# Attention and two gated layers on one core: the first chunk of tokens as plain float32 matmuls, and x of the second layer through the weights' buffers

## The chip, the cores and the metric

The kernel runs on one core of a Trainium2 chip. The metric is the device time of one execution in microseconds (us); less is better. Engines are called as in the profile: PE (TensorE, matmuls), PEld (its weight loads), DVE (VectorE), ACT (ScalarE), POOL (GpSimd) and SP (SyncE, which here only issues transfers).

## The reference

Block-causal attention, then two dense layers. Inputs are drawn as float32 or, where the host keeps them in double precision, float64.

```python
def _attn_ref(q, k, v):                       # q, k, v: (4, 8, 576, 64)
    scores = scale * np.matmul(q, k.transpose(0, 1, 3, 2))
    mask = block_i >= block_j                 # blocks of 64 positions
    scores = np.where(mask, scores, -1000000000.0)
    ...
    return np.matmul(attn, v)

def _moe_ref(x, w1, w2, w3, w_out):           # x: 2304 x 512, w: 512 x 768
    h = np.maximum(np.maximum(x @ w1, x @ w2), x @ w3)
    return h @ w_out                          # 768 x 512

def _moe2_ref(x, w_gate, w_val, w_out):       # 512 x 1536, 1536 x 512
    gate = 1.0 / (1.0 + np.exp(-(x @ w_gate)))
    return gate * (x @ w_val) @ w_out
```

## The kernel before

**Weights.** All weights arrive in 64-bit words, 128 x 512 words a piece (512 KB): 24 pieces `wa` of layer 1 (18 of the experts w1 to w3, 6 of w_out) and 36 pieces `wb` of stage 2, as the second layer is called here. A piece is turned into float32 on chip: ACT rescales the high word (L671), DVE shifts the low word (L675) and joins the two (L679). The joined float32 value then lies in every second 32-bit word of the tile. Since matmuls run in the fast type fp32r, which keeps fewer bits, every operand is split: ACT casts the high part (L691), DVE subtracts it for the low part (L90, tile `w` or `WB`). A product takes three matmuls: high x high, high x low, low x high (L511 to L513 for the experts, L549 to L551 for the projection with w_out, L1002 to L1004 for gate and value, L982 to L984 for the output).

**Where the pieces lie.** Single pieces go through a ring of four buffers (`raw_p`, tile `wraw`), which comes free with the low part. In front, 15 pieces of layer 1 are loaded three at a time into the places of weights that are not made yet (`land_unit`, tile `wland`, 1.5 MB; five units, u from 2 to 6).

**Layer 1 and attention.** Attention is 32 jobs (a batch and a pair of heads, once for its first 256 tokens and once for the other 320). Layer 1 goes in eight chunks: four of 256 tokens, then four of 320. Chunk i needs the four jobs that make its tokens, and runs beside the next four. Per chunk there are 18 groups `experts(i, f, w)` (f of six blocks of h, w of three matrices; 12 matmuls each), their maximum (`larger`: ACT copies the first, L520, DVE takes the maximum with the second and third, L522), the split of h (`high_h` on ACT, L533, `low_h` on DVE), and 4 groups `project(i, d, fs)` of 18 matmuls, whose result goes to DRAM (`x2d`).

**The order.** Jobs, weights and chunks are written as `Op`s with an engine, a cost, what they wait for, the ring they take a buffer from and a due time. `plan()` runs a list scheduler over them: it gives each engine the ready Op that is due first, with 1.9 us from a load's end to its reader and 370 GB/s on the wire. `run_plan()` then emits everything in the order of the planned starts, and that order is kept on PE, DVE, ACT and SP. The chip waits where the plan was wrong; it doesn't reorder.

**Stage 2.** Six chunks of 384 tokens, 12 steps f each. A step is 24 matmuls into `ps_g` and `ps_v`, a sigmoid (ACT), a product `gv` (DVE, L1009) and its split, and 9 matmuls for the output. `get_x(c, t)` loads the x of a chunk from `x2d` into a tile of its own, `xraw` (L961, 768 KB), DVE casts its four parts (L85, `XT<-xraw`), and POOL makes the low parts (L90, `XE` or `XT`). The pieces of `wb` are loaded and split by the plan; the matmuls of stage 2, the loads of x and its casts are emitted behind it with due times of their own (`at`), and a buffer of a ring is handed out in the order in which it is asked for.

Of the kernel before, what the change touches and what calls it, by code (L numbers as in the profile page):

```python
# [25 lines left out]
N2 = 384  # L26
# [29 lines left out]
    "w2late": 10.0,  # L56
    "lean": 0.0,
    "cold": 45.0,
    "evac2": 30,
    "olag": 3.731,  # L60
}

RING = {"qk": 2, "v": 4, "s": 3, "t": 2, "o": 1, "m": 2, "w": 8, "raw": 4, "tmp": 4, "st": 3}


@with_exitstack
def block_attention_moe_moe(ctx: ExitStack, tc, k1, q1, v1, k2, q2, vt, wa, wb, out):
# [91 lines left out]
    def plan():  # L159
# [23 lines left out]
        def ready(o):  # L183

            if any(d.end is None for d in o.deps):
                return None
            t = max([d.end + lat + (1.9 if d.eng == "S" else 0.25 * (d.eng == "P")) for d in o.deps] + [0.0])
            if o.ring:
                r = rings.setdefault(o.ring, [])
                n = RING[o.ring]  # L190
                if len(r) >= n:
                    old = r[len(r) - n]
                    if any(d.end is None for d in old.frees) or not old.frees:
                        return None
# [19 lines left out]
        while left:  # L214
# [289 lines left out]
    def experts(i, f, w):  # L504
# [126 lines left out]
    for i in range(2 * B):  # L631
        c = i // B
        mm = [(f, w) for f in range(NF1) for w in range(3)] + [(NF1, d) for d in range(KD)]
        n_v = ends[i + 1] + 1 - vn if i + 1 < 2 * B else 0
        v0 = vn
        for n, (f, w) in enumerate(mm):
            mpos[i, f, w] = t
            t += (12 if f < NF1 else 18) * CM[c]
            if i == 0 and f < NF1:
                t += P["wgap"]  # L640
            while vn < v0 + n_v and (vn - v0 + 1) * (len(mm) - P["tail"]) <= (n + 1) * n_v:
                t = visit(t)
                vn += 1
    TB = t

    def build():
# [15 lines left out]
        def pieces(ld, land, dest, before=(), ring=None, due=None):  # L662
# [80 lines left out]
        def job(j):  # L743
# [109 lines left out]
            old = last_mm.get(ci - 2, [])  # L853
            xh = Op(*both(n, True), lambda e: split(j, 0, e), [p] + old)
            xl = Op(*vec(n), lambda: split(j, 1, None), [xh])
            xh.late = xl.late = pos("P") + P["xsplit"]
            p.frees = [xl]
            x_ops.setdefault(ci, []).append(xl)

        def chunk(i):  # L860
# [27 lines left out]
            for d in range(KD):  # L888
                pos = mpos[i, NF1, d]
                deps = hl_ops[:-1] if d == 0 else hl_ops  # L890
                if i == 0:
                    deps = deps + after(*[conv[k] for k in range(18, 24 if d else 23)])
                if d == 0:
                    o = pe("M", 15 * CM[c], lambda: project(i, 0, range(NF1 - 1)), deps, pos, ring="m")
                    o2 = pe("M", 3 * CM[c], lambda: project(i, 0, (NF1 - 1,)), hl_ops + (list(conv[23]) if i == 0 else []), pos + 0.01)
                    done = [o, o2]
                else:
                    o = pe("M", 18 * CM[c], lambda d=d: project(i, d, range(NF1)), deps, pos, ring="m")
                    done = [o]
                if i == 2 * B - 1:  # L900
# [3 lines left out]
                st.late = pos + 18 * CM[c] + P["evac"]  # L904
                o.frees = [st]
# [175 lines left out]
```

## Time and profile before

| | us |
|---|---|
| median of 3 runs (lowest, highest) | 977.79 (977.33, 979.42) |
| the profiled execution | 980.47 |
| its span in the trace | 978.7 |
| PE busy | 939.3 (96%) |
| DVE busy | 468.0 (48%) |
| ACT busy | 389.4 (40%) |
| POOL busy | 101.0 (10%) |

Times below are counted from the span's start. PE's clock is given as the granted clock: 1.00 is 2.4 GHz, 0.50 is 1.2 GHz. An engine runs its own instructions in order, so an instruction that waits holds up all behind it. A row of the waits says which engine, tile and line waited for which engine, tile and line, how long in all, how often, and the longest. Matmuls overlap in the pipe, so their pace is read from start to start and not from their duration.

### The profile page before, as it was taken

To read this page: it belongs to the slowest core of one execution; us is meant where nothing else is said; L and a number is where in the kernel's file an instruction comes from. 1 tells how busy PE (TensorE), PEld (TensorE's weight loads), DVE (VectorE), ACT (ScalarE), POOL (GpSimd) and SP (SyncE) were. 2 spreads that over 40 slices of the span, in tenths; PEclk is the share of its full clock that TensorE was granted. 3 is DMA by queue.
4 is the path that set the end of the run, shared out by engine and by line. 5 is a ranking of instruction groups with operands and counts; after the bars stand their busy time and mean duration, and the time that the engine had idled before them with its cause. 6 is when DMAs were issued, how large, how long until landed. Compare 5 with 4: busy or idle time off the path is not lost.

```text
span 978.7 us, 14918 instructions
## 1 busy us (share of the span) xinstructions
PE 939.3 (96%) x5912; PEld 874.5 (89%) x5912; DVE 468.0 (48%) x1145; ACT 389.4 (40%) x923; POOL 101.0 (10%) x102
## 2 busy tenths in 40 slices
PE   4787999999999999999889999999999999999998
PEld 3587999999999999999879999999999999999997
DVE  7899665688676687676689701002002001100100
ACT  5975434366565466564546512111112111111211
POOL 0000000000000000000013113113113113111111
PEclk9897999999999999999999999999999999999999
DMA  9911122221212214101667401001001000000000
GB/s 310 366 55 44 61 90 71 81 76 60 97 59 83 65 59 175 59 1 26 227 195 255 138 1 65 1 1 63 3 1 35 31 1 1 33 1 1 33 1 33
DMA packets 37350, 72.27 MB, mean 74 GB/s; under 512 B 5792, under 2 KB 19104, under 8 KB 37280
## 3 DMA queue, kind: packets, MB, share of 16 engines
q1 hardware_dynamic: 37280, 71.32, 22.1%
q8 instruction: 46, 0.75, 0.3%
q14 instruction: 24, 0.20, 0.1%
HBM read 61.87 MB, written 9.44 MB: 73 GB/s over the span
## 4 chain that ended last, share of the span: by engine, by line
PE 86%; DMA 6%; DVE 6%; ACT 1%; issue 1%; SPq 1%; ACTq 0%; DVEq 0%
PE ps_m L511 6%; PE ps_m L512 6%; PE ps_m L513 6%; PE ps_out L983 5%; PE ps_out L984 5%; PE ps_g L1002 5%; PE ps_g L1004 5%; PE ps_v L1002 5%; PE ps_g L1003 5%; PE ps_v L1004 5%; PE ps_v L1003 5%; PE ps_out L982 5%; PE ps_o L478 4%; PE ps_t L440 3%; PE ps_m L549 2%; PE ps_m L551 2%
## 5 line engine op out<-in xcount | busy, mean ns | idle before, releaser
L1009 DVE TENSOR_TENSOR gv<-ps_v,sg 128x384 f32<-128x384 f32 x72 | 40.1, 556 | 342.1 <-PE ps_v L1004 341.6
L511 PE MATMUL ps_m<-XT,w 128*128 128x256 f32 (+1 forms) x576 | 177.4, 308 | 10.0 <-DVE m L522 8.2
L513 PE MATMUL ps_m<-XT,w 128*128 128x256 f32 (+1 forms) x576 | 172.2, 299 | 3.5 <-DVE w L90 3.5
L512 PE MATMUL ps_m<-XT,w 128*128 128x256 f32 (+1 forms) x576 | 172.0, 299 | 0.4 <-DVE XT L90 0.4
L511 PEld LDWEIGHTS ps_m<-XT,w 128*128 128x128 f32 x576 | 110.3, 192 | 14.2 <-DVE m L522 7.8
L513 PEld LDWEIGHTS ps_m<-XT,w 128*128 128x128 f32 x576 | 110.5, 192 | 3.9 <-DVE w L90 3.9
L1007 ACT ACTIVATE sg<-ps_g 128x384 f32<-128x384 f32 x72 | 35.4, 492 | 195.2 <-PE ps_g L1004 195.2
L512 PEld LDWEIGHTS ps_m<-XT,w 128*128 128x128 f32 x576 | 110.5, 192 | 1.2 <-DVE XT L90 0.5
L90 POOL TENSOR_TENSOR HR<-gv,HR 128x384 fp32r<-128x384 f32 x72 | 74.0, 1028 | 342.0 <-ACT HR L1013 342.0
L1013 ACT CAST HR<-gv 128x384 fp32r<-128x384 f32 x72 | 37.0, 513 | 149.5 <-DVE gv L1009 149.5
L387 ACT ACTIVATE E<-ps_s,nm 128x256 f32<-128x256 f32 (+3 forms) x128 | 66.3, 524 | 39.2 <-DVE nm L382 38.6
L90 POOL TENSOR_TENSOR XE<-xraw,XT 128x384 fp32r<-128x384 f32 x12 | 13.1, 1111 | 512.6 <-DVE XT L85 512.6
L1004 PE MATMUL ps_g<-XT,w 128*128 128x384 f32 x192 | 64.8, 337 | 0.0
L1002 PE MATMUL ps_g<-XT,w 128*128 128x384 f32 x192 | 64.7, 337 | 0.0
L1002 PE MATMUL ps_v<-XT,w 128*128 128x384 f32 x192 | 64.1, 334 | 0.0
L1004 PE MATMUL ps_v<-XT,w 128*128 128x384 f32 x192 | 64.1, 334 | 0.0
L549 PE MATMUL ps_m<-HR,w 128*128 128x256 f32 (+1 forms) x192 | 60.7, 316 | 1.2 <-ACT HR L533 1.0
L522 DVE TENSOR_TENSOR m<-ps_m,m 128x256 f32<-128x256 f32 (+1 forms) x96 | 43.6, 454 | 37.4 <-PE ps_m L513 36.5
L478 PE MATMUL ps_o<-PT,v 128*64 128x320 f32 (+3 forms) x448 | 54.4, 375 | 6.1 <-ACT PT L81 3.9
L550 PE MATMUL ps_m<-HR,w 128*128 128x256 f32 (+1 forms) x192 | 58.8, 306 | 1.0 <-DVE HR L90 1.0
L551 PE MATMUL ps_m<-HR,w 128*128 128x256 f32 (+1 forms) x192 | 58.9, 307 | 0.5 <-DVE w L90 0.5
L984 PE MATMUL ps_out<-w,HR 128*128 128x512 f32 x144 | 57.0, 395 | 0.0
(116 smaller groups left out, 2151.3 us busy)
## 6 DMA issues: line engine op xcount, KB each, us to landing
wraw<-in_wb_dram SPq DMA_DIRECT2D x36, 512.0 KB, 4.4
qk<-in_k_dram SPq DMA_DIRECT2D x16, 576.0 KB, 4.1
wland<-in_wa_dram SPq DMA_DIRECT2D x5, 1536.0 KB, 17.4
v<-in_vt_dram SPq DMA_DIRECT2D x16, 320.0 KB, 3.0
wraw<-in_wa_dram SPq DMA_DIRECT2D x9, 512.0 KB, 6.5
xraw<-x2d SPq DMA_DIRECT2D x6, 768.0 KB, 4.7
out_dram<-osb SPq DMA_DIRECT2D x18, 256.0 KB, 2.2
qk<-in_k_dram SPq DMA_DIRECT2D x13, 256.0 KB, 3.1
```

The source lines that it names most:

```text
L90: (V if e == "V" else G).tensor_tensor(out=out, in0=a, in1=b, op=ALU.subtract)
L387: A.activation(E[h][:, e : e + 128 * (t + 1)], j.s[h, t], AF.Exp, bias=j.nm[:, c : c + 1], scale=1.0, accum_out=j.sm[:, c : c + 1],)
L478: T.matmul(j.o[rows(h), d : d + n], j.v[:, h, k, :], PT[:, h, c : c + n], start=(k == 0), stop=(k == len(parts) - 1), skip_group_check=True,)
L511: T.matmul(ps, wt[:, 0, w, k], xh[:, k], start=(k == 0), stop=False)
L512: T.matmul(ps, wt[:, 0, w, k], xl[:, k], start=False, stop=False)
L513: T.matmul(ps, wt[:, 1, w, k], xh[:, k], start=False, stop=(k == KD - 1))
L549: T.matmul(ps, wh, hh, start=(f == 0), stop=False)
L551: T.matmul(ps, wl, hh, start=False, stop=(f == NF1 - 1))
L984: T.matmul(ps, gl[:, ct], wh, start=False, stop=(f == NF2 - 1))
L1002: T.matmul(ps, w[:, 0, i, k], xh[:, k], start=(k == 0), stop=False)
L1003: T.matmul(ps, w[:, 0, i, k], xl[:, k], start=False, stop=False)
L1004: T.matmul(ps, w[:, 1, i, k], xh[:, k], start=False, stop=(k == KD - 1))
```

## The change

- Chunk 0 of layer 1 uses plain float32 matmuls, whose weights are the joined words (every second word of `wland` or `wraw`): `experts32` takes 4 matmuls for 12, `project32` 6 for 18. Its x and h stay whole in float32, in the place of the first three jobs' q and k (tile `qkv`). So chunk 0 needs no cast and no low part of weights, x or h. It needs the joins alone.
- Casts and low parts of the weights are made for chunk 1. A piece's buffer comes free when chunk 0's matmuls have read it too.
- Six units of three pieces are loaded ahead, not five. The ring of raw buffers has five places, not four; a tile of probabilities (`PT`) is a little smaller for it.
- The planner counts 2.7 us from a load to its reader and 350 GB/s.
- `get_x` has no tile of its own: x of a stage 2 chunk comes in two transfers of two parts each, through the ring `raw_p`, which the 36 pieces of `wb` use before.

```diff
-RING = {"qk": 2, "v": 4, "s": 3, "t": 2, "o": 1, "m": 2, "w": 8, "raw": 4, "tmp": 4, "st": 3}
+RING = {"qk": 2, "v": 4, "s": 3, "t": 2, "o": 1, "m": 2, "w": 8, "raw": 5, "tmp": 4, "st": 3}
...
-            t = max([d.end + lat + (1.9 if d.eng == "S" else 0.25 * (d.eng == "P")) for d in o.deps] + [0.0])
+            t = max([d.end + lat + (P["wire"] if d.eng == "S" else 0.25 * (d.eng == "P")) for d in o.deps] + [0.0])
...
+    x32 = first[:, :1024].rearrange("p (k n) -> p k n", k=KD)
+
+    def h32(f):
+        return first[:, 1024 + 256 * f : 1280 + 256 * f]
+
+    def value(i):
+        if not wide:
+            return f32(lands[i])
+        return lands[i].rearrange("p (n w) -> p n w", w=2)[:, :, 1].bitcast(F32)
+
+    def experts32(f, w):
+        ps = pm.tile([128, 512], F32, tag="m", name="ps_m")[:, :256]
+        x = value(3 * f + w)
+        for k in range(KD):
+            T.matmul(ps, x[:, 128 * k : 128 * k + 128], x32[:, k], start=(k == 0), stop=(k == KD - 1))
+        pss[0, f, w] = ps
+
+    def project32(d, fs):
+        if 0 in fs:
+            pss[0, d] = pm.tile([128, 512], F32, tag="m", name="ps_m")[:, :256]
+        for f in fs:
+            wo = value(18 + f)[:, 128 * d : 128 * d + 128]
+            T.matmul(pss[0, d], wo, h32(f), start=(f == 0), stop=(f == NF1 - 1))
+
     def larger(i, f, w):
         n = CH1[i // B][1]
-        m = tmp_p.tile([128, N2], F32, tag="tmp", name=f"m{w}")[:, :n]
+        if i == 0 and w == 2:
+            m = h32(f)
+        else:
+            m = tmp_p.tile([128, N2], F32, tag="tmp", name=f"m{w}")[:, :n]
...
-        for u in range(2, 7):
+        for u in range(1, 7):
...
-                    deps = x_ops[i] + (list(conv[3 * f + w]) if i == 0 else [])
-                    o = pe("M", 12 * CM[c], lambda f=f, w=w: experts(i, f, w), deps, pos, ring="m")
+                    deps = x_ops[i] + (ready32[3 * f + w] if i == 0 else list(conv[3 * f + w]) if i == 1 else [])
+                    if i == 0:
+                        o = pe("M", mcost(i, f), lambda f=f, w=w: experts32(f, w), deps, pos, ring="m")
+                        landed[3 * f + w].frees.append(o)
+                    else:
+                        o = pe("M", 12 * CM[c], lambda f=f, w=w: experts(i, f, w), deps, pos, ring="m")
...
-    xraw = mb.tile([128, KD, N2], F32, name="xraw")
...
     def get_x(c, t):
-        at(t - 30)
-        nc.sync.dma_start(out=xraw, in_=x2d[:, :, N2 * c : N2 * c + N2])
         xh, xl = xbuf(c)
-        at(t - 20)
-        for k in range(KD):
-            copy(ENG["sx"], xh[:, k], xraw[:, k])
-            sub(ENG["sl"], xl[:, k], xraw[:, k], f32(xh[:, k]))
+        n = 1 + wide
+        for k0 in range(0, KD, n):
+            at(t - 30)
+            x = raw_p.tile([128, PC * n], U32, tag="raw", name="xraw").bitcast(F32)
+            x = x[:, : N2 * n].rearrange("p (k n) -> p k n", k=n)
+            nc.sync.dma_start(out=x, in_=x2d[:, k0 : k0 + n, N2 * c : N2 * c + N2])
+            at(t - 20)
+            for k in range(n):
+                copy(ENG["sx"], xh[:, k0 + k], x[:, k])
+                sub(ENG["sl"], xl[:, k0 + k], x[:, k], f32(xh[:, k0 + k]))
```

The change adds lines, so a line has another number in it: L675 becomes L711 (shift), L679 L715 (join), L90 L92 (low part), L522 L552 (maximum), L85 L87 (cast).

The order shows the change at three places. **DVE around the first maximum of chunk 0** (`m<-ps_m`; K, L and Q are the split of job 5's keys and queries). Before:

```order
L90 TENSOR_TENSOR w<-wland,w 128x512
L90 TENSOR_TENSOR L<-qk,K 128x2x256
L346 SCALAR_TENSOR_TENSOR Q_104<-qk,Q_104 64x512
L675 TENSOR_SCALAR wraw<-wraw 128x512
L85 CAST K<-qk 128x2x256
L679 SCALAR_TENSOR_TENSOR wraw<-wraw 128x512
L90 TENSOR_TENSOR L<-qk,K 128x2x256
L675 TENSOR_SCALAR wraw<-wraw 128x512
L90 TENSOR_TENSOR w<-wraw,w 128x512
L679 SCALAR_TENSOR_TENSOR wraw<-wraw 128x512
L346 SCALAR_TENSOR_TENSOR Q_103<-qk,Q_103 64x512
L522 TENSOR_TENSOR m_513<-ps_m,m_494 128x256
```

In the change:

```order
L715 SCALAR_TENSOR_TENSOR wland<-wland 128x512 x2
L711 TENSOR_SCALAR wland<-wland 128x512 x2
L715 SCALAR_TENSOR_TENSOR wland<-wland 128x512 x2
L711 TENSOR_SCALAR wland<-wland 128x512 x2
L715 SCALAR_TENSOR_TENSOR wland<-wland 128x512 x2
L711 TENSOR_SCALAR wland<-wland 128x512 x2
L715 SCALAR_TENSOR_TENSOR wland<-wland 128x512 x2
L552 TENSOR_TENSOR m_487<-ps_m,m_470 128x256
L711 TENSOR_SCALAR wland<-wland 128x512 x2
L715 SCALAR_TENSOR_TENSOR wland<-wland 128x512
L92 TENSOR_TENSOR L<-qk,K 128x2x256
L348 SCALAR_TENSOR_TENSOR Q_104<-qk,Q_104 64x512
```

The low parts of weights (`w<-wraw`, `w<-wland`) that stood ahead of the maximum are gone from here; fourteen shifts and joins of the units stand there, and job 5's keys come after them.

**DVE at the end of layer 1** (the first two maxima of chunk 7, the last of layer 1, among pieces of `wb`). Before:

```order
L675 TENSOR_SCALAR wraw<-wraw 128x512
L679 SCALAR_TENSOR_TENSOR wraw<-wraw 128x512
L675 TENSOR_SCALAR wraw<-wraw 128x512
L679 SCALAR_TENSOR_TENSOR wraw<-wraw 128x512
L90 TENSOR_TENSOR WB_5570<-wraw,WB_5570 128x512
L522 TENSOR_TENSOR m_5669<-ps_m,m_5647 128x320
L675 TENSOR_SCALAR wraw<-wraw 128x512
L90 TENSOR_TENSOR WB_5570<-wraw,WB_5570 128x512
L522 TENSOR_TENSOR m_5689<-ps_m,m_5669 128x320
```

In the change:

```order
L711 TENSOR_SCALAR wraw<-wraw 128x512
L715 SCALAR_TENSOR_TENSOR wraw<-wraw 128x512
L711 TENSOR_SCALAR wraw<-wraw 128x512
L552 TENSOR_TENSOR m_5455<-ps_m,m_5437 128x320
L92 TENSOR_TENSOR WB_5357<-wraw,WB_5357 128x512
L715 SCALAR_TENSOR_TENSOR wraw<-wraw 128x512
L711 TENSOR_SCALAR wraw<-wraw 128x512
L552 TENSOR_TENSOR m_5478<-ps_m,m_5455 128x320
```

One low part has moved from ahead of the first maximum to behind it.

**DVE and SP at the step to stage 2** (the last maxima of chunk 7, the cast of x from `xraw`, and the product `gv` of stage 2). DVE before:

```order
L90 TENSOR_TENSOR HR<-m_5949,HR 128x320
L90 TENSOR_TENSOR w<-wraw,w 128x512
L522 TENSOR_TENSOR m_5990<-ps_m,m_5969 128x320
L85 CAST XT<-xraw 128x384 x3
L90 TENSOR_TENSOR w<-wraw,w 128x512
L85 CAST XT<-xraw 128x384
L675 TENSOR_SCALAR wraw<-wraw 128x512
L679 SCALAR_TENSOR_TENSOR wraw<-wraw 128x512
L522 TENSOR_TENSOR m_6016<-ps_m,m_5990 128x320
```

DVE in the change, the last twelve rows up to the first product:

```order
L92 TENSOR_TENSOR w<-wraw,w 128x512
L711 TENSOR_SCALAR wraw<-wraw 128x512
L715 SCALAR_TENSOR_TENSOR wraw<-wraw 128x512
L711 TENSOR_SCALAR wraw<-wraw 128x512
L92 TENSOR_TENSOR w<-wraw,w 128x512
L715 SCALAR_TENSOR_TENSOR wraw<-wraw 128x512
L87 CAST XT<-xraw 128x384 x2
L92 TENSOR_TENSOR w<-wraw,w 128x512
L87 CAST XT<-xraw 128x384 x2
L92 TENSOR_TENSOR w<-wraw,w 128x512
L87 CAST XT<-xraw 128x384 x4
L1071 TENSOR_TENSOR gv<-ps_v,sg 128x384 x11
```

The cast of x stood ahead of the last maximum of chunk 7; now the last maximum is 43 rows above the first cast (row 879 against 928 of the engine, some of them several instructions), and all the pieces stand between. SP before:

```order
L568 DMA x2d<-x2s 128x128
L961 DMA xraw<-x2d 128x4x384
L106 DMA wraw<-in_wb_dram 128x512
L568 DMA x2d<-x2s 128x128
L568 DMA x2d<-x2s 128x64
L568 DMA x2d<-x2s 128x128
L106 DMA wraw<-in_wb_dram 128x512 x3
L568 DMA x2d<-x2s 128x128
L568 DMA x2d<-x2s 128x64
L568 DMA x2d<-x2s 128x128
L106 DMA wraw<-in_wb_dram 128x512 x14
L961 DMA xraw<-x2d 128x4x384
```

SP in the change, the end of its loads:

```order
L108 DMA wraw<-in_wb_dram 128x512 x2
L598 DMA x2d<-x2s 128x128
L598 DMA x2d<-x2s 128x64
L598 DMA x2d<-x2s 128x128
L108 DMA wraw<-in_wb_dram 128x512 x6
L1024 DMA xraw<-x2d 128x2x384 x11
L1052 DMA out_dram<-osb 128x512 x3
```

The load of the first x stood ahead of 32 of the 36 pieces; now it stands behind them all.

## Rows read from the trace of the kernel before

**Rows 1.** Windows: stretch, length, busy of PE, PEld, DVE, ACT, POOL, clock, DMA share, GB/s

```profile
0.00:36.50 36.50, 21.84 (x96) 16.01 (x96) 30.16 (x88) 26.36 (x75) 0.70 (x6) 0.86 0.97 342
36.50:60.00 23.50, 16.39 (x126) 14.59 (x125) 21.12 (x52) 19.38 (x44) 0.00 (x0) 1.00 0.67 207
60.00:92.00 32.00, 25.95 (x186) 23.24 (x184) 31.73 (x82) 19.21 (x52) 0.00 (x0) 0.93 0.12 34
92.00:103.10 11.10, 11.08 (x70) 10.53 (x70) 6.18 (x17) 3.00 (x10) 0.00 (x0) 0.73 0.36 109
103.10:472.70 369.60, 369.60 (x2814) 346.24 (x2812) 255.33 (x694) 198.62 (x513) 0.00 (x0) 1.00 0.23 75
472.70:507.80 35.10, 30.20 (x183) 29.45 (x183) 28.75 (x58) 21.04 (x39) 0.51 (x1) 0.90 0.61 196
507.80:527.70 19.90, 17.08 (x96) 15.83 (x95) 18.89 (x30) 8.56 (x16) 9.30 (x8) 0.91 0.67 219
527.70:978.70 451.00, 447.18 (x2352) 418.63 (x2352) 75.84 (x130) 93.26 (x180) 90.44 (x88) 1.00 0.09 30
```

**Rows 2.** Waits, 36.5 to 104 us: total, times, longest

```profile
PE ps_m L513 <- DVE w L90: 3.5, 2, 2.8
PE ps_m L511 <- DVE m L522: 3.3, 2, 1.8
```

**Rows 3.** Waits, 472.7 to 507.8 us

```profile
DVE wraw L675 <- DMA wraw<-in_wb_dram: 5.6, 4, 2.8
PE ps_m L511 <- DVE m L522: 4.9, 3, 2.9
```

**Rows 4.** Windows: four microseconds behind the wait at 475.7

```profile
476.00:480.00 4.00, 3.78 (x17) 3.38 (x17) 3.03 (x7) 3.26 (x6) 0.00 (x0) 0.61 0.56 164
```

**Rows 5.** Timeline of PE, two places: start, duration, line, tiles, shape

```profile
103.11 0.28 PE L511 MATMUL ps_m<-XT,w 128*128 128x256 f32 x1
103.23 0.28 PE L512 MATMUL ps_m<-XT,w 128*128 128x256 f32 x1
...
343.46 0.44 PE L478 MATMUL ps_o<-PT,v 128*64 128x320 f32 x2
...
343.73 0.44 PE L478 MATMUL ps_o<-PT,v 128*64 128x320 f32 x2
```

**Rows 6.** Groups by line, PE's weight loads, whole span

```profile
L511 PEld LDWEIGHTS ps_m<-XT,w 128*128 128x128 f32 x576 | 110.3, 192 | 14.2 <-DVE m L522 7.8 <-issue 3.5 <-ACT m L520 1.6
```

**Rows 7.** Timeline of DVE beside stage 2

```profile
547.32 0.42 DVE L675 TENSOR_SCALAR wraw<-wraw 128x512 uint32<-128x512 uint32 x1
547.66 0.68 DVE L90 TENSOR_TENSOR w<-wraw,w 128x512 fp32r<-128x512 f32 x1
548.26 0.68 DVE L679 SCALAR_TENSOR_TENSOR wraw<-wraw 128x512 uint32<-128x512 uint32 x1
548.86 0.41 DVE L675 TENSOR_SCALAR wraw<-wraw 128x512 uint32<-128x512 uint32 x1
```

**Rows 8.** Timeline of DVE, two places

```profile
12.72 0.17 DVE L394 TENSOR_SCALAR rc<-sm 128x4 f32<-128x4 f32 x1
...
39.44 0.43 DVE L85 CAST K<-qk 128x512 fp32r<-128x512 f32 x1 [0.53 <-DMA qk<-in_k_dram]
```

**Rows 9.** Timeline of DVE, x of stage 2

```profile
506.79 1.90 DVE L85 CAST XT<-xraw 128x384 fp32r<-128x384 f32 x3 [0.17 <-PE ps_m L512]
...
510.04 1.14 DVE L85 CAST XT<-xraw 128x384 fp32r<-128x384 f32 x1
```

**Rows 10.** Timeline of POOL, x of stage 2

```profile
511.26 1.12 POOL L90 TENSOR_TENSOR XE<-xraw,XT 128x384 fp32r<-128x384 f32 x1 [0.29 <-DVE XT L85]
```

**Rows 11.** Timeline of PE, last expert matmul, second step of stage 2

```profile
507.47 0.31 PE L513 MATMUL ps_m<-XT,w 128*128 128x320 f32 x1
...
527.73 0.45 PE L1002 MATMUL ps_g<-XT,WB 128*128 128x384 f32 x1 [0.39 <-ACT x2s L81]
```

**Rows 12.** Timeline of SP, loads of the last weight pieces

```profile
537.63 11.06 SPq L106 DMA_DIRECT2D wraw<-in_wb_dram  x6
```

More of the change, by code (lines that the diff above doesn't have):

```diff
@@ L57 @@
     "lean": 0.0,
+    "wire": 2.7,
+    "rate": 350e3,
     "cold": 45.0,
@@ L126, in block_attention_moe_moe @@
     E4 = ap1.tile([128, S], F32, name="E4")
-    PT = ap1.tile([128, 2, 1408], F32, name="PT")
+    PT = ap1.tile([128, 2, 1344], F32, name="PT")
     EO = [0, 128, 0, 384]
@@ L239, in plan @@
             if e == "S" and o.size:
-                wire[0] = max(wire[0], t) + o.size / 370e3
+                wire[0] = max(wire[0], t) + o.size / P["rate"]
                 o.end = wire[0]
@@ L690, in pieces @@
                 last = [Op(*vec(PC), join, [p, s])]
+            ld.values = getattr(ld, "values", [])
+            ld.values.append(last)
             h = Op(*act(PC), lambda: A.copy(dest()[0], value()), last + list(before), ring=ring)
@@ L853, in job @@
             old = last_mm.get(ci - 2, [])
-            xh = Op(*both(n, True), lambda e: split(j, 0, e), [p] + old)
-            xl = Op(*vec(n), lambda: split(j, 1, None), [xh])
-            xh.late = xl.late = pos("P") + P["xsplit"]
+            if ci == 0:
+                xl = Op(*both(n, True), lambda e: copy(e, x32[:, j.p], j.o[:, :n]), [p] + jobs[0].prep)
+            else:
+                xh = Op(*both(n, True), lambda e: split(j, 0, e), [p] + old)
+                xl = Op(*vec(n), lambda: split(j, 1, None), [xh])
+                xh.late = pos("P") + P["xsplit"]
+            xl.late = pos("P") + P["xsplit"]
             p.frees = [xl]
@@ L876, in chunk @@
                     else:
-                        e = Op(*vec(n), lambda f=f, w=w: larger(i, f, w), [o, m[-1]], ring="tmp")
+                        old = after(jobs[1].prep, jobs[2].prep) if i == 0 and w == 2 else []
+                        e = Op(*vec(n), lambda f=f, w=w: larger(i, f, w), [o, m[-1]] + old,
+                               ring=None if i == 0 and w == 2 else "tmp")
                         m[-1].frees = [e]
-                    e.late = pos + 12 * CM[c] + P["evac"]
+                    e.late = pos + mcost(i, f) + P["evac"]
                     o.frees = [e]
                     m.append(e)
-                hh = Op(*act(n), lambda f=f: high_h(i, f), [m[-1]] + oldp + (after(*[j.prep for j in jobs[:3]]) if i == 0 else []))
+                if i == 0:
+                    hl_ops.append(m[-1])
+                    last_mm[i] = [o]
+                    continue
+                hh = Op(*act(n), lambda f=f: high_h(i, f), [m[-1]] + oldp)
                 hl = Op(*vec(n), lambda f=f: low_h(i, f), [hh])
@@ L890, in chunk @@
                 deps = hl_ops[:-1] if d == 0 else hl_ops
-                if i == 0:
-                    deps = deps + after(*[conv[k] for k in range(18, 24 if d else 23)])
+                if i < 2:
+                    deps = deps + after(*[(ready32, conv)[i][k] for k in range(18, 24 if d else 23)])
+                run = project if i else lambda _, d, fs: project32(d, fs)
+                cost = mcost(i, NF1) / NF1
                 if d == 0:
-                    o = pe("M", 15 * CM[c], lambda: project(i, 0, range(NF1 - 1)), deps, pos, ring="m")
-                    o2 = pe("M", 3 * CM[c], lambda: project(i, 0, (NF1 - 1,)), hl_ops + (list(conv[23]) if i == 0 else []), pos + 0.01)
+                    o = pe("M", (NF1 - 1) * cost, lambda: run(i, 0, range(NF1 - 1)), deps, pos, ring="m")
+                    o2 = pe("M", cost, lambda: run(i, 0, (NF1 - 1,)), hl_ops + ([] if i > 1 else list((ready32, conv)[i][23])), pos + 0.01)
                     done = [o, o2]
                 else:
-                    o = pe("M", 18 * CM[c], lambda d=d: project(i, d, range(NF1)), deps, pos, ring="m")
+                    o = pe("M", NF1 * cost, lambda d=d: run(i, d, range(NF1)), deps, pos, ring="m")
                     done = [o]
+                if i == 0:
+                    for k in range(18, 24):
+                        landed[k].frees.extend(done)
                 if i == 2 * B - 1:
```

15 lines of the change are left out of this document (11 added, 4 removed).

## The prediction

> **What bounds the kernel now.** I read the windows by stage first, to see which stretches of TensorE (PE) are not full [rows 1]. From 103.1 us (the start of chunk 1) to 472.7 PE is busy in all 369.6 us, and in stage 2, from 527.7 on, in 447 of 451: nothing that the change does there on other engines can be seen in the time. The gaps lie in chunk 0 (36.5 to 103.1: busy 16.4 + 26.0 + 11.1 = 53.4 of 66.6, so 13.2 idle), at the end of layer 1 (472.7 to 507.8: 4.9 idle) and in the step to stage 2 (507.8 to 527.7: 2.8 idle). Next the waits. In chunk 0 PE waits for VectorE (DVE): for a low part of a weight and for a maximum [rows 2], and DVE is busy in 31.7 of 32 us of the middle stretch, so it is the bound there. At the end of layer 1 PE waits for a maximum again, which stands on DVE behind weight pieces of stage 2 that wait for their loads [rows 3]. Last the granted clock. Around each such wait it falls from 2.4 to 1.2 GHz for some microseconds [rows 4]; by the windows' mean clock this costs 0.07 x 32.0 + 0.27 x 11.1 = 5.2 us in chunk 0 and 0.10 x 35.1 = 3.5 at the end of layer 1. So chunk 0 wastes 13.2 + 5.2 = 18.4 us, and the end of layer 1 8.4.
>
> **Part 1: chunk 0 in plain float32.** PE's price first. An fp32r matmul of 256 columns follows the one before in 0.12 us [rows 5], and chunk 0 has 18 x 12 + 72 = 288 of them: 34.3 us at 0.119. A plain float32 matmul is seen only in the attention's apply: 0.27 us from pair to pair at 320 columns, where each matmul shows two records [rows 5]; that is 0.2155 a record at 256 columns and 0.431 a matmul. 96 of them take 41.4 us. **PE gets 7.1 us more work**, so 18.4 - 7.1 = 11.3 us is the most that this part can give, if it left no gap at all.
>
> DVE's price: a weight piece costs a shift of 0.34, a join of 0.60 and a low part of 0.60, back to back [rows 7], 1.55 together. Counted in the order, DVE's work from 12.7 us on, up to where both orders are alike [rows 8], to the first maximum of chunk 1 hardly shrinks: 24 shifts, 24 joins and 24 low parts (37.2 us) stand in both; only six low parts of h go (2.0) and some of x, against smaller pieces of other work, 78.3 us for 79.1. What changes is who waits. All 24 low parts now stand behind the chunk's first maximum, due only when chunk 1 needs them. But the units come in first: 17 shifts and 17 joins stand ahead of the first maximum (9 shifts, 8 joins and 8 low parts before), and all six units ahead of job 5's K and Q; K landed at 39.4 even behind five [rows 8]. DVE comes past job 5's Q after 35.1 us of work, at 12.7 + 35.1 = 47.8 if it never waits. In PE's order 4 expert groups stand ahead of job 5's scores, so it then has 14 of 18 left (14 x 4 x 0.431 = 24.1), the projection (24 x 0.431 = 10.3) and about two thirds of the attention in this stretch (53.4 busy, less 34.3 of chunk 0, less 5.2 of clock, is 14; two thirds are 9): 91.2. DVE has 43.2 left: 91.0. The two bounds meet, and neither will be kept: I add 2 us for the units (DVE idles 2.7 between 36.5 and 92 today [rows 1]) and 3 for PE and DVE waiting in turn. Chunk 1 starts at 96 and not 103.1: **-7**. The ends are -2 (DVE's sum alone decides, 0.8 less work and a little less waiting) and -11.3.
>
> The weight operand is now every second word. The nearest row is LDWEIGHTS of 128x128 from packed words, 192 ns on average [rows 6], under the 215 ns of a float32 record; no PE read at a stride is in the trace. ACT and DVE read the same words at that stride today without a price (low part of a weight from the wide tile 0.60, the same as others). I take 0, and keep twice the packed time as the other end (a rival below). The Trainium skill ("SBUF — State Buffer", section "Door 1: The DMA port swizzle") states 16-byte lines that give full bandwidth from two accesses in a line, and a penalty for each crossing to a new line; words 8 bytes apart make just two accesses in a line, so by it the price would be 0 too, on the very edge. No run here shows it yet.
>
> **Part 2: x through the raw ring.** This is the term that decides. Today the load of stage 2's first x is issued at 462.1, well ahead of most weight pieces, into a tile of its own, and its casts stand in the middle of the pieces: 506.8 and 510.0 on DVE, the last low part on POOL done at 512.4 [rows 9, 10]. So PE can begin stage 2 early; the second of its 72 steps begins at 527.73, 19.95 after the end of the last expert matmul at 507.78 [rows 11]. In the change the x tiles are the 37th and later tiles of a ring in which the 36 weight pieces come first. The order shows it on all three engines: SP has all 36 loads ahead of x, ACT all casts ahead of the first sigmoid, and DVE 16 shifts, 16 joins, 16 low parts and one of h between chunk 7's last maximum and the first cast of x: 16 x (0.34 + 0.60 + 0.60) + 0.34 = 25.1 us. Loads allow it: the last six follow each other at 11.06/6 = 1.84 us with four buffers [rows 12], 7.4 a turn, so 1.5 with five, about DVE's own pace.
>
> PE's cover in this time is the projection of chunk 7, 72 x 0.119 x 320/256 = 10.7 us; then it stands still, about 15 us, and afterwards runs at half clock, as behind every such gap [rows 4]. The maximum is done 0.6 after the last expert matmul, the casts begin at +25.7, casts and POOL's low parts take 5.6 as today (506.8 to 512.4) and the last matmuls of ps_g half a microsecond; ps_v's 12 follow at 2 x 0.119 x 384/256, 4.3 together. The second step begins at +36 for +19.95: **+16**. Floor 13 (no half clock, x's low parts 1 us quicker); top 22 (loads at today's 1.84 a piece add 16 x 0.29 = 4.6, and one turn of the ring before x another 1 or 2).
>
> **Part 3: the end of layer 1.** Five raw buffers for four, and no 768 KB of x on the wire between the pieces (2.3 us at the 342 GB/s of the first 36.5 us [rows 1]). In the order the maximum that PE waited 2.9 us for stands behind shift, join, shift and no longer behind a low part too. Of the 8.4 us I take a good half, **-4.5**; the ends are +2 (a planner that expects slower loads places a maximum behind another late piece) and -8.4.
>
> The table of attention probabilities, the planner's latency and its rate cost nothing by themselves: they change the order, which is counted above. The 369.6 full microseconds cover whatever moved there; they hold the same matmuls.
>
> **Sum.** 980.5 (the profiled execution) - 7 - 4.5 + 16 = 985. That execution is 2.7 above the median of the runs, 977.8; against the median the forecast is **982.3**.
>
> **Rivals.**
> - **Slower by more** (0.20). The early waits stay: units of 1.5 MB are all or nothing, the sixth unit is now ahead of job 5's loads (4.6 us more at 342 GB/s), so DVE's sum starts late. Part 1 gives 0 to 2 and part 2 18 to 20: 980.5 - 1 - 3 + 19 - 2.7 = 993. For it: DVE's sum is unchanged. Against: PE's chain has 18.4 us of waste to lose.
> - **Strided weight loads bind PE** (0.04). At twice 0.19 a record takes 0.38, a matmul 0.76: 96 x 0.33 = 32 us more in chunk 0, of which DVE's slack hides little: about 1010. For it: nothing shows the stride on PE. Against: none of the other engines pays.
> - **The parts balance** (0.13): -9, -6 and +15, within 2 us (0.2%, about what a measurement of this kernel can tell) of no change.
> - **Faster** (0.17). DVE stops being the bound of chunk 0: with the low parts behind the maxima PE runs there without a gap and at full clock, -11. Its place is the stretch from 36.5 to chunk 1, its price that stretch's waste; it decides where PE idles less than about 2 us there, with the end of layer 1 clean too (-8.4) and part 2 at 14: 980.5 - 11 - 8.4 + 14 - 2.7 = 972.4. For it: PE's and DVE's bounds both allow 91. Against: they meet, so every early wait counts.
> - That the x loads go early after all is excluded by the order.
>
> The forecast itself, slower by 2 to 10 us, has 0.46; slower in all 0.46 + 0.20 + 0.04 = 0.70, same 0.13, faster 0.17. The range 974 to 993 leaves out the strided case and the tails of the rivals on either side, some 2 in 10; the forecast alone would give 980 to 988.
>
> **What would show it.** Right: chunk 1's first matmul at 94 to 99; DVE still near full in chunk 0, PE's waits there on maxima and joins, none on a low part; float32 matmuls 0.43 apart; the first cast of x some 25 us behind the last expert matmul; a PE gap of 12 to 18 us after chunk 7's projection, which waits for x, and a granted clock near 0.5 behind it; no gap over 1 us from 472 on before that. Wrong: x cast beside the last experts; float32 matmuls well over 0.43; chunk 1 before 92 or after 102; or PE gaps between 103 and 472, where I count none.

## The result, and the profile after

The change takes 983.96 us (median; 983.57 to 986.57), the kernel before beside it 977.56. The ratio is 1.0064, 95% interval 1.0048 to 1.0081: slower by some 6.3 us, by 4.7 to 7.9. The profiled execution took 984.26 us, its span is 982.5.

The windows of the change by stage: start of chunk 0 (a round 36.5), the middle, the last stretch before chunk 1 (96.3), chunks 1 to 6, chunk 7's expert groups, most of the step to stage 2 (its second step begins at 531.69), stage 2 (columns as in [rows 1]):

```profile
36.50:60.00 23.50, 20.52 (x93) 17.03 (x91) 22.82 (x57) 15.26 (x37) 0.00 (x0) 0.80 0.65 204
60.00:84.50 24.50, 24.50 (x137) 21.45 (x137) 23.15 (x61) 15.21 (x40) 0.00 (x0) 1.00 0.24 68
84.50:96.30 11.80, 11.80 (x63) 10.23 (x62) 9.54 (x23) 7.27 (x19) 0.00 (x0) 1.00 0.26 80
96.30:460.70 364.40, 364.40 (x2778) 341.18 (x2777) 256.98 (x696) 200.12 (x517) 0.00 (x0) 1.00 0.23 72
460.70:492.60 31.90, 31.90 (x220) 31.90 (x219) 29.44 (x60) 22.81 (x41) 0.00 (x0) 1.00 0.79 270
492.60:530.00 37.40, 16.84 (x89) 15.18 (x88) 34.25 (x61) 23.59 (x40) 6.98 (x6) 0.69 0.85 273
530.00:982.50 452.50, 448.73 (x2361) 420.20 (x2359) 54.01 (x95) 77.92 (x155) 91.62 (x91) 1.00 0.05 17
```

[rows 1] cut before at 472.7, which is inside chunk 7. Cut at the start of chunk 7 (467.3), with as many matmuls in each window as above, the windows of before are:

```profile
103.10:467.30 364.20, 364.20 (x2778) 341.02 (x2777) 253.72 (x691) 197.62 (x511) 0.00 (x0) 1.00 0.22 72
467.30:507.80 40.50, 35.59 (x220) 34.67 (x219) 30.36 (x61) 22.04 (x41) 0.51 (x1) 0.92 0.65 211
```

Two stretches got better and one worse. In chunk 0 PE is full from 60 us on, and chunk 1 starts at 96.3. Chunks 1 to 6 take the same. Chunk 7's groups have no gap and no lost clock and take 31.9 us for 40.5, where before had 4.9 us idle. In the step to stage 2 PE does 16.84 us of work in 37.4, at a mean clock of 0.69. PE's timeline shows the place, the last expert matmul and then the first of stage 2:

```profile
492.26 0.31 PE L515 MATMUL ps_m<-XT,w 128*128 128x320 f32 x1
...
502.82 0.31 PE L581 MATMUL ps_m<-HR,w 128*128 128x320 f32 x1
522.64 0.66 PE L1064 MATMUL ps_g<-XT,WB 128*128 128x384 f32 x1 [19.51 <-DVE XT L87]
524.27 0.69 PE L1065 MATMUL ps_g<-XE,WB 128*128 128x384 f32 x1 [0.96 <-POOL XE L92]
...
528.65 0.52 PE L1064 MATMUL ps_v<-XT,WB 128*128 128x384 f32 x1
...
531.69 0.33 PE L1064 MATMUL ps_g<-XT,WB 128*128 128x384 f32 x1
```

PE waits 19.5 us for the cast of x. The second step begins at 531.69, 39.1 behind the last expert matmul's end; before that was 19.95 [rows 11]. DVE in that time works on weight pieces, with one low part of h between them:

```profile
492.61 0.49 DVE L552 TENSOR_TENSOR m<-ps_m,m 128x320 f32<-128x320 f32 x1
493.02 0.42 DVE L711 TENSOR_SCALAR wraw<-wraw 128x512 uint32<-128x512 uint32 x1
...
503.56 0.43 DVE L711 TENSOR_SCALAR wraw<-wraw 128x512 uint32<-128x512 uint32 x1 [0.50 <-DMA wraw<-in_wb_dram]
...
507.55 0.42 DVE L711 TENSOR_SCALAR wraw<-wraw 128x512 uint32<-128x512 uint32 x1
508.08 0.69 DVE L715 SCALAR_TENSOR_TENSOR wraw<-wraw 128x512 uint32<-128x512 uint32 x1
...
510.42 0.42 DVE L711 TENSOR_SCALAR wraw<-wraw 128x512 uint32<-128x512 uint32 x1
510.76 0.68 DVE L92 TENSOR_TENSOR w<-wraw,w 128x512 fp32r<-128x512 f32 x1
...
522.14 0.62 DVE L87 CAST XT<-xraw 128x384 fp32r<-128x384 f32 x2
523.28 2.23 DVE L87 CAST XT<-xraw 128x384 fp32r<-128x384 f32 x2
```

From the last maximum (492.61) to the first cast are 29.5 us, where [rows 9] had the casts among the maxima. DVE is not alone in holding x up. SP's timeline has the loads of x behind those of all pieces:

```profile
517.09 4.92 SPq L1024 DMA_DIRECT2D xraw<-x2d  x3
```

These three landed 3.6 to 4.5 us after their issue, the first at 521.56, only 0.6 ahead of the cast. So the place of x on the DMA queue and its place on DVE bind at almost the same time, and by these times moving only one of them could not have won much.

All runs are read by four lengths below, each from PE's timeline: the start of chunk 1, from there to the end of chunk 7's last expert matmul, from there to the first output matmul of stage 2, and from there to the span's end.

| run | chunk 1 starts | to the last expert | to the first output | to the end |
|---|---|---|---|---|
| before | 103.11 | 404.67 | 28.40 | 442.52 |
| before, again (e8) | 101.83 | 403.61 | 28.50 | 442.52 |
| the change | 96.32 | 396.25 | 47.44 | 442.47 |
| e1, change, x in its own place | 95.30 | 397.92 | 27.43 | 442.34 |
| e2, before, x through the ring | 99.93 | 399.24 | 55.23 | 442.34 |
| e3, change, no float32, five units | 100.48 | 396.64 | 48.27 | 442.35 |
| e4, change, old planner | 97.14 | 397.86 | 49.85 | 442.47 |
| e5, e1 without float32, five units | 100.30 | 397.07 | 25.73 | 442.52 |
| e6, e1 with four buffers | 97.63 | 398.54 | 28.82 | 442.34 |
| e7, e1 with five units | 105.86 | 396.97 | 26.84 | 442.51 |
| e9, e1 without float32, six units | 100.24 | 397.58 | 25.79 | 442.34 |
| e10, before, x in its own place | 101.39 | 403.95 | 29.41 | 442.51 |
| e11, e1, planner at 3.5 us | 94.46 | 396.25 | 27.17 | 442.34 |
| e12, before, new planner | 100.99 | 400.26 | 29.10 | 442.52 |

### The profile page after: what moved, and what is told of

It is laid out like the page before. It is cut to its first block, busy times and chain, and to the rows that moved or that the text cites. A ratio compares the mean times of both kernels' runs of the same rounds, so it can differ in the third digit from the quotient of the medians.

```text
span 982.5 us, 14745 instructions
## 1 busy us (share of the span) xinstructions
PE 939.7 (96%) x5816; PEld 872.9 (89%) x5816; DVE 460.5 (47%) x1137; ACT 387.7 (39%) x915; POOL 99.3 (10%) x102
## 4 chain that ended last, share of the span: by engine, by line
PE 91%; DMA 4%; SPq 2%; DVE 2%; issue 1%; POOL 0%; ACT 0%; DVEq 0%; ACTq 0%
PE ps_m L513 7%; PE ps_m L514 7%; PE ps_m L515 7%; PE ps_out L1045 5%; PE ps_out L1046 5%; PE ps_g L1065 5%; PE ps_g L1066 5%; PE ps_v L1064 5%; PE ps_v L1065 5%; PE ps_v L1066 5%; PE ps_g L1064 5%; PE ps_out L1044 5%; PE ps_o L480 5%; PE ps_t L442 3%; PE ps_m L533 3%; PE ps_s L367 2%
## 5 line engine op out<-in xcount | busy, mean ns | idle before, releaser
L513 PE MATMUL ps_m<-XT,w 128*128 128x320 f32 (+1 forms) x504 | 154.4, 306 | 0.0
L515 PE MATMUL ps_m<-XT,w 128*128 128x320 f32 (+1 forms) x504 | 150.0, 298 | 0.0
L514 PE MATMUL ps_m<-XT,w 128*128 128x320 f32 (+1 forms) x504 | 149.9, 297 | 0.0
L92 POOL TENSOR_TENSOR HR<-gv,HR 128x384 fp32r<-128x384 f32 x72 | 72.9, 1013 | 340.7 <-ACT HR L1075 340.7
L513 PEld LDWEIGHTS ps_m<-XT,w 128*128 128x128 f32 x504 | 95.3, 189 | 1.7 <-issue 1.0
L514 PEld LDWEIGHTS ps_m<-XT,w 128*128 128x128 f32 x504 | 95.4, 189 | 0.7
L515 PEld LDWEIGHTS ps_m<-XT,w 128*128 128x128 f32 x504 | 95.2, 189 | 0.0
L389 ACT ACTIVATE E<-ps_s,nm 128x256 f32<-128x256 f32 (+3 forms) x128 | 66.3, 525 | 39.1 <-DVE nm L384 38.3
L92 POOL TENSOR_TENSOR XE<-xraw,XT 128x384 fp32r<-128x384 f32 x12 | 13.3, 1134 | 527.7 <-DMA xraw<-x2d 521.4
L552 DVE TENSOR_TENSOR m<-ps_m,m 128x320 f32<-128x320 f32 (+1 forms) x90 | 41.2, 458 | 35.2 <-PE ps_m L515 34.1
L1046 PE MATMUL ps_out<-w,HR 128*128 128x512 f32 x144 | 57.0, 395 | 0.0
L1045 PE MATMUL ps_out<-w,HR 128*128 128x512 f32 x144 | 56.8, 395 | 0.0
L480 PEld LDWEIGHTS ps_o<-PT,v 128*64 128x64 f32 x448 | 31.4, 141 | 28.6 <-DVE PT L87 6.4
L384 DVE TENSOR_REDUCE nm<-ps_s 128x1 f32<-128x256 f32 (+3 forms) x128 | 55.7, 466 | 1.5 <-ACT E L389 0.4
```

The source lines that it names most:

```text
L92: (V if e == "V" else G).tensor_tensor(out=out, in0=a, in1=b, op=ALU.subtract)
L384: V.tensor_reduce(out=j.nm[:, c : c + 1], in_=j.s[h, j.tiles[i]], axis=AX.X, op=ALU.max, negate=True)
L389: A.activation(E[h][:, e : e + 128 * (t + 1)], j.s[h, t], AF.Exp, bias=j.nm[:, c : c + 1], scale=1.0, accum_out=j.sm[:, c : c + 1],)
L480: T.matmul(j.o[rows(h), d : d + n], j.v[:, h, k, :], PT[:, h, c : c + n], start=(k == 0), stop=(k == len(parts) - 1), skip_group_check=True,)
L513: T.matmul(ps, wt[:, 0, w, k], xh[:, k], start=(k == 0), stop=False)
L514: T.matmul(ps, wt[:, 0, w, k], xl[:, k], start=False, stop=False)
```

## The experiments

The runs were made in four sittings, and the kernel before ran in each: its medians there were 978.56 (e1 to e4), 976.36 (e5 to e8), 978.11 (e9 to e11) and 977.54 (e12). Medians of different sittings are compared to some 2 us, ratios to their intervals.

**e1: x out of the ring.** The rest of the change stays. x is loaded into the tile of its low part, and POOL writes the low part over it.

```diff
 def get_x(c, t):
     xh, xl = xbuf(c)
+    at(t - 30)
+    nc.sync.dma_start(out=f32(xl), in_=x2d[:, :, N2 * c : N2 * c + N2])
+    at(t - 20)
+    for k in range(KD):
+        copy(ENG["sx"], xh[:, k], f32(xl[:, k]))
+        sub(ENG["sl"], xl[:, k], f32(xl[:, k]), f32(xh[:, k]))
```

> The change, but x of stage 2 does not go through the weights' ring: it is loaded straight into the place of its low part, and the low part is made there. Theory A (x stands behind the pieces on DVE, which costs stage 2's start 19 us): the PE gap of 19.5 us is gone and the time is 984 - 19 = 965 (963 to 968; the load of 768 KB is back among the pieces and may cost up to 2). Rival B (stage 2 waits for the weight pieces themselves and x only marks the place): the gap becomes a wait for a weight, 975 to 984.

964.18 us, ratio to before 0.9851 (0.9832 to 0.9870), in the range of theory A. SP's timeline of e1 has the load of the first x early again:

```profile
454.46 0.56 SPq L1020 DMA_DIRECT2D XE<-x2d  x1
```

And DVE's timeline of e1 has the casts behind it:

```profile
492.76 1.98 DVE L87 CAST XT<-XE 128x384 fp32r<-128x384 f32 x4
494.66 1.51 DVE L715 SCALAR_TENSOR_TENSOR wraw<-wraw 128x512 uint32<-128x512 uint32 x1
496.09 0.48 DVE L552 TENSOR_TENSOR m<-ps_m,m 128x320 f32<-128x320 f32 x1
```

The casts stand ahead of chunk 7's last maximum again, stage 2's first output comes 27.4 us behind the last expert, and the weight pieces, which are as many as in the change, hold PE up no more than before (idle 2.5 of 19.1 us from 493.2 on, before 2.8 of 19.9 [rows 1]). Theory A holds, rival B falls: some 20 us lay in x's place in the order, on the DMA queue and on DVE together.

**e2: the same part alone.** The kernel before with `get_x` of the change, and nothing else.

> The kernel before, with nothing changed but x through the raw ring (four buffers). Theory A: the start of stage 2 loses 19 us as in the change, and some 4 more since four buffers bring a piece only every 1.84 us; the 768 KB load is no longer between the pieces, which may give back up to 3: 977.6 + 17 to 23 = 994 to 1001. Rival B: within 5 us of 978.

1002.85 us, 1.0241 (1.0218 to 1.0264): 24 us lost, and a little more than A expected. The step takes 55.2 us for 28.4, that is 26.8 more, while chunk 1 to the last expert takes 4 to 5 less than before (x's load of 768 KB and its casts are gone from there). The trace is of the fastest of five executions, 998.54; what the others lost on top, 2 to 7 us, is in no trace. DVE's groups from 497 to 537 us:

```profile
L675 DVE TENSOR_SCALAR wraw<-wraw 128x512 uint32<-128x512 uint32 x18 | 7.7, 425 | 6.7 <-DMA wraw<-in_wb_dram 6.7
```

With four buffers and the old planner DVE waits 6.7 us for loads there; the change, with five and the new one, waits 1.1.

**e3: no float32.** Chunk 0 as before (three matmuls, five units); ring, buffers and planner of the change.

```diff
-for u in range(1, 7):
+for u in range(2, 7):
...
-deps = x_ops[i] + (ready32[3 * f + w] if i == 0 else list(conv[3 * f + w]) if i == 1 else [])
+deps = x_ops[i] + (list(conv[3 * f + w]) if i == 0 else [])
```

> The change without the float32 chunk 0 and without the sixth unit: three matmuls a product there, five raw buffers, the planner's new numbers and x through the ring stay. Theory A (float32 gave the 6.8 us in chunk 0): chunk 1 starts at 103 and the time is 984 + 7 = 991 (988 to 993). Rival C (the fifth buffer and the planner's numbers gave chunk 0 its gain): 983 to 985, chunk 1 at 96 to 98.

987.25 us, 1.0092 (1.0076 to 1.0109): 3 above the change, between the two theories. Chunk 1 starts at 100.5. So chunk 0's float32 together with the sixth unit gives 4.2 us at that point, by one profile each, and not the 6.8 between the first two profiles; the medians say 3.3.

**e4: the planner's old numbers.** Two lines of the table set back to 1.9 us and 370 GB/s.

> The change with the planner's old numbers (1.9 us from a load to its reader, 370 GB/s). Theory A (the numbers only shift the order a little): 984 within 2. Rival D (the 8.4 us at the end of layer 1 come from maxima placed for slower loads): the waits of 3 us at the end of layer 1 are back, 987 to 993.

989.08 us, 1.0104 (1.0087 to 1.0121), 4 to 5 above the change and in the range of rival D. The numbers are worth something, which the prediction denied, though not by waits of 3 us at the end of layer 1 as rival D had it (PE's longest from 455 to 500 us is 0.7): chunk 1 starts 0.8 later, the last expert comes 1.6 later from there, the step takes 2.4 more.

**e8: before, once more.** No edit.

> The kernel before once more, for its profile. If the granted clock varies from run to run, chunk 1 starts at about 100 and not at 103.1, with the same gaps in chunk 0 and a clock nearer 1 from 84 to 103 us. If 103.1 is what the kernel needs, it is 103 again.

Chunk 1 starts at 101.8, between the two numbers. The windows behind the last long wait of chunk 0, before:

```profile
84.00:92.00 8.00, 6.23 (x27) 5.19 (x27) 7.95 (x20) 5.34 (x14) 0.00 (x0) 0.74 0.00 0
92.00:103.00 11.00, 10.98 (x70) 10.43 (x70) 6.18 (x17) 3.00 (x10) 0.00 (x0) 0.73 0.36 109
```

The same of e8:

```profile
84.00:92.00 8.00, 6.55 (x28) 5.16 (x27) 7.92 (x21) 5.33 (x15) 0.00 (x0) 0.59 0.00 0
92.00:103.00 11.00, 11.00 (x79) 10.55 (x80) 6.27 (x16) 2.72 (x8) 0.00 (x0) 0.84 0.39 121
```

And those of e2, whose chunk 0 is the kernel before's too:

```profile
84.00:92.00 8.00, 5.97 (x30) 4.83 (x30) 7.93 (x22) 5.26 (x16) 0.00 (x0) 0.84 0.00 0
92.00:100.00 8.00, 8.00 (x69) 7.55 (x69) 5.52 (x14) 2.40 (x7) 0.00 (x0) 1.00 0.41 131
```

The wait ahead of these stretches is the same in all three (2.8 us for a low part, at 84); the granted clock behind it is not, and chunk 1 starts at 99.9, 101.8 or 103.1 with it.

**e5, e9, e7: float32 and the sixth unit apart.** All three are e1 with the one, the other or both of its parts for chunk 0 taken back.

> As the run with x in its own place, but without the float32 chunk 0 (and five units as in the kernel before): three matmuls a product there. It gives float32's worth free of the loss at stage 2. Theory A, corrected (worth 3.3, as between the change and the run without float32; the other 3 us of the 6.8 between the two profiles were the granted clock): 964.2 + 3.3 = 967.5 (966 to 969). Rival (worth 6.8 as the profiles show): 971.

> As the run without float32 and with x in its own place, but with six units in front. With float32 the sixth unit was worth 9.5 us (973.6 against 964.2). Theory E (the sixth unit pays only together with float32, since without it a buffer is free as soon as its low part is made): within 3 us of 968. Theory F (the sixth unit brings the gain by itself and float32 adds nothing): 958 to 964.

> As the run with x in its own place, but five units of weights in front instead of six. If the gap of 2.8 us ahead of chunk 0's second group comes from the shifts and joins of units ahead of the first maximum, it gets smaller and chunk 1 starts at 93 to 95: 962 to 964. If the data only come later by it: 964 to 967.

| | five units | six units |
|---|---|---|
| three matmuls | 967.95 (e5; 0.9909, 0.9890 to 0.9928) | 967.68 (e9; 0.9900, 0.9884 to 0.9916) |
| float32 | 973.64 (e7; 0.9967, 0.9954 to 0.9980) | 964.18 (e1; 0.9851, 0.9832 to 0.9870) |

e5 came out as its corrected theory A said. Without float32 the sixth unit does nothing (theory E). With five units float32 costs 5.7 us; with six it gives 3.5, by the medians (4.8 by the ratios). Both expectations of e7 missed: chunk 1 starts at 105.9. The loads of layer 1's pieces on SP's timeline in e7 (start, duration, count):

```profile
9.04 3.23 SPq L108 DMA_DIRECT2D wraw<-in_wa_dram  x5
12.62 8.90 SPq L108 DMA_DIRECT2D wland<-in_wa_dram  x5
66.38 4.34 SPq L108 DMA_DIRECT2D wraw<-in_wa_dram  x2
73.70 0.93 SPq L108 DMA_DIRECT2D wraw<-in_wa_dram  x2
```

The same in e1:

```profile
9.62 0.90 SPq L108 DMA_DIRECT2D wraw<-in_wa_dram  x2
10.57 12.53 SPq L108 DMA_DIRECT2D wland<-in_wa_dram  x6
23.14 4.90 SPq L108 DMA_DIRECT2D wraw<-in_wa_dram  x2
65.04 0.33 SPq L108 DMA_DIRECT2D wraw<-in_wa_dram  x1
```

A raw buffer of a float32 chunk 0 stays taken until its matmuls have read it and the low part is made. With five units four pieces wait for that until 66 to 74 us, with six only one. PE is busy in 7.65 of the 12 us from 60 to 72 in e7, and in all 12 in e1. But what PE waits for there is not a weight: its longest wait from 60 to 73 us in e7 is 2.7 us for a tile of the attention on DVE. So why the two parts pay only together is argued here from the late pieces and not shown; no run has them alone.

**e6: four buffers, e10: a control, e12: the planner alone.** e6 is e1 with `"raw": 4`; e10 is the kernel before with e1's `get_x`; e12 the kernel before with 2.7 us and 350 GB/s.

> As the run with x in its own place, but with four raw buffers. Theory A (the fifth buffer keeps the maxima of chunk 7 from standing behind late loads; its worth is at the end of layer 1): gaps of 1 to 3 us from 466 to 493 come back, stage 2 starts as far behind the last expert matmul as before; 966 to 970. Rival (the gain at the end of layer 1 came from the 768 KB load being gone, and the buffers do nothing): 964.

> The kernel before, with x loaded straight into the place of its low part instead of a tile xraw. A control for the runs above: if that way of loading x is itself worth something (another pace of POOL's low parts), the time moves by more than 2 us; else 976 to 979, and stage 2's first output matmul starts 28.4 us behind the last expert matmul as before.

> The kernel before with nothing but the planner's new numbers (2.7 us, 350 GB/s): four buffers, five units, x in its own tile, no float32. The run without float32 and with x in its own place is 10 us faster than the kernel before and differs from it by these numbers and the fifth buffer. Theory G (the numbers are the gain: maxima no longer stand behind pieces that have not landed; the time from chunk 1's start to the last expert matmul falls from 404 to 397 or 399): 968 to 972. Rival (the fifth buffer is the gain): 975 to 979.

e6: 966.23 us, 0.9890 (0.9870 to 0.9909), in the range of theory A, but its gaps did not come back: PE's longest wait from 455 to 500 us is 0.8. The loss against e1 is 2.1 us by the medians. The two profiles are 4.3 apart (e6's is of its slowest execution, 969.14), of which 2.3 lie in chunk 0, 1.4 in the step and only 0.6 from chunk 1 to the last expert. e10: 978.72, 1.0001 (0.9992 to 1.0010): loading x in place is worth nothing by itself (the step takes 29.4, 1.0 more than was said), so what e1 shows is x's place in the order. e12: 974.30, 0.9960 (0.9946 to 0.9974), between the theories: the planner's numbers give 3 to 4 us alone, nearly all from chunk 1 to the last expert (400.3 for 403.6 to 404.7). e5 is 8 to 9 us below the kernel before, so some 5 of them belong to the fifth buffer or to the two together; the buffer was not tried alone on the kernel before.

**e11: a better version.** e1 with `"wire": 3.5`.

> As the run with x in its own place, with the planner counting 3.5 us from a load to its reader and not 2.7. The change's numbers gave 5 us against the old ones (989.1 to 984.0). If the plan is still too early for the loads, 961 to 964; if 2.7 was about right, 964 to 968.

962.61 us, 0.9839 (0.9825 to 0.9852): the lowest median of all, 15.5 us below the kernel before. Against e1 it is 1.6 lower by medians of two sittings, and the intervals of the ratios overlap, so that gain is not shown. Chunk 1 to the last expert is 396.25, as full as in the change.

## Why the prediction was right, and where its sizes were off

The sign, the mechanism and the range held: 982.3 was forecast for 983.96. That it came so near is in part luck: part 2 was sized 3 us too small and part 3 3 to 4 too small, and the two errors cancel. The three terms, against the profile of before that they were read from and against e8's:

| term | forecast | by the profile before | by e8 |
|---|---|---|---|
| part 1, start of chunk 1 | -7 | -6.8 | -5.5 |
| part 3, chunk 1 to the last expert | -4.5 | -8.4 | -7.4 |
| part 2, step to stage 2 | +16 | +19.0 | +18.9 |
| sum | +4.5 | +3.8 | +6.0 |

**Part 1.** Chunk 1 starts at 96.3, 96 was said. PE's waits were where they were said to be: for a maximum behind the units' joins once (2.98 us at 46.9), for attention, none for a low part. From the waits of the change, 36 to 97 us:

```profile
PE ps_m L533 <- DVE m L552: 3.0, 1, 3.0
PE ps_o L480 <- DVE PT L87: 1.0, 1, 1.0
```

PE goes on at 46.9 behind that wait, where 47.8 was said, and is busy from there on:

```profile
46.90:53.00 6.10, 6.10 (x21) 5.38 (x22) 5.94 (x15) 2.47 (x5) 0.00 (x0) 0.51 0.37 114
53.00:96.30 43.30, 43.30 (x237) 37.60 (x236) 39.21 (x98) 27.32 (x75) 0.00 (x0) 1.00 0.26 75
```

So "3 for PE and DVE waiting in turn" was clock: 0.49 x 6.1 = 3.0 us, and nothing is lost behind it. In place of the "2 us for the units" stood work: 15 groups were left and not 14 (1.7), and the attention took some 1 more than its estimate. PE's bound alone decided, with DVE busy in 45.1 of these 49.4 us. And the other side was mis-sized: the 18.4 us of waste of before were one execution's. The clock's share in it (5.2) varies; e8 and e10, with the same order in chunk 0, start chunk 1 at 101.8 and 101.4. So the profile of before, 2.7 us above its median, carried about half of that surplus (1.3 us, against e8) in the term that was measured from it, and float32 with the sixth unit is worth 3.3 to 3.8 us by the medians, not 7. That the two pay only together was not seen at all.

The price of a float32 matmul held: 16 records follow from 60.27 to 63.72, 0.2156 each, 0.431 a matmul, with weights at a stride. PE's timeline of the change:

```profile
60.27 3.62 PE L533 MATMUL ps_m<-qkv,wland 128*128 128x256 f32 x16
63.72 0.49 PE L442 MATMUL ps_t<-ident,E 128*128 128x128 f32 x3
```

The group of its weight loads in the change, from 53 to 96 us, where the clock is full:

```profile
L533 PEld LDWEIGHTS ps_m<-qkv,wland 128*128 128x128 f32 x112 | 21.3, 196 | 2.4 <-issue 0.3 <-DVE m L552 0.2
```

The weight loads took 196 ns, under the 0.2155 us of a record, against 189 from packed words in the change's chunks 1 to 6 (the 192 of [rows 6] mixes clocks). Plain float32 took its price with them, so the stride cost the time nothing. The Trainium skill ("SBUF — State Buffer", section "Door 1: The DMA port swizzle") wants at least two accesses to a line of 16 bytes for full bandwidth, and words 8 bytes apart make two. The trace agrees but for the 7 ns, which the matmuls hide.

**Part 2.** Right in kind, 3 us short, by the step "16 x (0.34 + 0.60 + 0.60) + 0.34 = 25.1". DVE took 29.1 from the first shift (493.02) to the cast. The waits that the profile lists make 2.0 of the 4.0 (loads 1.1, ACT's rescale 0.7, a cast 0.2); most of the rest is DVE's own. A join that directly follows its own shift starts 0.52 to 0.53 behind it (507.55 and 508.08), and an instruction on another piece 0.34 behind (510.42 and 510.76). Seven of the 16 joins stand so, 1.3 us; [rows 7], from which the 0.34 was priced, has a low part in between. (Which shift is a join's own is taken from the order of the pieces.) So "16 x (0.34 + 0.60 + 0.60)" was too kind; the top of 22 held it. Two signs missed with it: the first cast came 29.6 us behind the last expert matmul, for some 25, and PE's gap was 19.5, for 12 to 18. Casts and low parts took 5.6 as forecast (522.14 to 527.78, from POOL's row below), and the clock was back at 530.6, so ps_v took 3.0 us and not 4.3, which gave 1.2 back.

```profile
522.72 5.06 POOL L92 TENSOR_TENSOR XE<-xraw,XT 128x384 fp32r<-128x384 f32 x4 [521.42 <-DMA xraw<-x2d]
```

**Part 3.** The step "a good half" failed: chunk 7 takes 8.6 us less, all of its waste. It also put the planner's numbers at nothing beyond the order, and the order was looked at in one place only. e2 shows that taking x's load and casts away is worth 4 to 5 us there by itself, and e12 that the planner's numbers are worth 3 to 4. Taken back from the change one at a time they cost only 1.7 (e1) and 1.6 (e4), so each does part of the other's work; which waits each of them mends was not traced.

**The rivals.** "Slower by more" had its part 2 (18 to 20) right and its part 1 wrong: the early waits did not stay. "Faster" was right that part 3 is emptied and chunk 0's PE runs full from 60 on; it needed part 1 at 11 and part 2 at 14, and they came at 5.5 to 6.8 and 19.

## What to carry to other kernels

The x that was put into the ring of buffers was served behind all that had asked for the ring before it, on the DMA queue and on DVE and ACT, which work on the ring's tiles. Before sharing a ring, look in the order for what then stands ahead of the new tile's load and ahead of its first reader: here 36 loads and, on DVE, 48 instructions, 20 us on a path that PE waits for. Giving x a place of its own turned 6 us lost into 14 won (e1). Price a term from one execution only after asking how much of it is granted clock: three executions with the same wait differed by 3 us in chunk 0. Two parts of a change may pay only together: test them as a square, not one by one. And read an instruction's price from a row where it stands among the same neighbours.

## What the runs showed of the hardware

- The granted clock behind the same wait (2.8 us, at 84) differs between executions: 0.74, 0.59 and 0.84 from 84 to 92 us in the profiles of before, e8 and e2, and 0.73, 0.84 and 1.00 behind that.
- Not each wait brings the clock down, as the prediction had it ("Around each such wait it falls"). Before, PE waited 3.3 us for maxima in two waits (1.75 us at 47.9, 1.54 at 51.8), and the clock stayed at 1.00 from 36.5 to 60 [rows 1].
- Behind the PE gap of 19.5 us the clock was 0.50 (1.2 GHz) from 522.6 to 530.5 and 0.99 from 530.5 to 540: matmuls of 384 columns stood 0.32 us apart (528.65 to 528.97), and 0.17 after.
- A plain float32 matmul of 256 columns shows two records of 0.2156 us, 0.431 together, for 0.12 of an fp32r matmul. Its weight load from words 8 bytes apart takes 196 ns for 189.
- On DVE a join of 128x512 words directly behind its own shift starts 0.52 to 0.53 us after it, and an instruction on another piece 0.34 (change, 493 to 522).
